# Opening loads ahead of the engines' arrivals at the barrier, and a shorter clock warm-up, in a decode attention kernel

## The chip, the cores and the metric

The kernel runs on one core of one Trainium2 chip. The metric is the device time of one execution in microseconds (us), and every number here is a device time or comes from a profile of one execution. "Span" is the time from the first to the last instruction that a profile shows; the device time is a little longer.

## The reference, cut to what matters

```python
xn = layernorm(x)                                    # x: 4 x 1 x 448
q  = (xn @ wq)                                       # 448 x 4096, 16 heads of 256
scores = einsum("bhqd,bhkd->bhqk", q, repeat(k_cache, 2)) * 256**-0.5
o  = einsum("bhqk,bhkd->bhqd", softmax(scores), repeat(v_cache, 2))
s  = o.reshape(4, 1, 4096) @ wo                      # 4096 x 448
h2 = gelu(layernorm(xn) @ w3) @ w4                   # 448 -> 1792 -> 448
out = x + s * silu(xn + h2)
```

The two caches are 4 x 8 x 8192 x 256 in bf16, 268 MB together; with the weights 279 MB are read for four output rows. (The reference's shifted branch with w1 and w2 is zero for a single position, so the kernel does not read those weights.) The caches are 32 tiles, one for each batch row and key head: 4 MB of K and 4 MB of V each.

## The kernel before

SyncE issues all large loads on one queue: wq, w3, w4, K of tiles 0 and 1, most of wo, and then K and V of the later tiles, each when its buffer comes free. ScalarE issues the load of x. A helper moves these first loads ahead of everything else on their engine, behind the instruction (a drain) with which the engine arrives at the barrier that opens the program:

```python
def begin_ahead(nc, loads):
    ...
    first = blocks[0].instructions
    for load in reversed(loads):
        at = next(n for n, i in enumerate(first)
                  if i.engine == load.engine and isinstance(i, mybir.InstDrain))
        first.insert(at + 1, load)          # behind the arrival
    blocks[0].instructions = first

def prog_sp(sp):
    ahead.append(sp.sem_inc(S["pause"], 1))     # two instructions
    ahead.append(take(sp, "pause"))             # ahead of wq
    ahead.append(sp.dma_start(vflat[1][:, 0:DK * HDH], A_wq...).then_inc(S["dwq"], 16))
    sp.dma_start(... B_w3 ...); sp.dma_start(... B_w4 ...)
    ...
    load_k(0); load_k(1)
    load_wo(NLATE, HQ, "dwo")
    for h in range(2, NH):
        load_k(h)                               # waits until tile h-2 of K is used up
        load_v(h - 2)

def prog_act(act):
    ahead.append(act.dma_start(x_sb[:, :], x2d).then_inc(S["dx"], 16))
```

TensorE first computes the small products of the prologue (q, the two layers of the MLP), then multiplies zeros to keep its clock up until the first tile of K has landed, and then works through the tiles:

```python
for i in range(NWARM):                          # NWARM = 14, the zero products
    pe.matmul(psv[0:PVW, 0:QW], pT[:, 0, 0:PVW], wq_sb[:, 0, 0:QW], start=True, stop=True)
...
def f_t(h, j):                                  # transposes of K, group j of 16
    if j == 0:
        take(pe, "dk%d" % (h % 2), 16)          # K of this tile has landed
    ...
def finish():                                   # after the last tile
    f_bc(h)
    ...                                         # rest of softmax, V of tiles 30 and 31
    f_direct(NPIECE - 1).then_inc(S["p_pv"], 1)
    take(pe, "dwl0", 16); f_o(LATE[0])
    take(pe, "v_ot");     f_o(range(HQ - REP, HQ))
    for i in range(1, len(LATE)):               # the last pieces of wo
        take(pe, "dwl%d" % i, 16)
        ins = f_o(LATE[i], i == len(LATE) - 1)
```

## Time and profile before

| | before |
|---|---|
| device time, first three runs | 653.57 us median (653.56 to 654.46) |
| profiled run: device time, span | 653.45 us, 652.0 us |
| wq issued, its first packet | 0.24 us, 1.26 us |
| x: load issued, cast starts | 0.21 us, 2.01 us |
| first tile, third K load issued | 30.07 us, 41.77 us |
| last packet of the stream | 648.80 us |

### The profile page before, as it was taken

Reading aid. Unit: us, or ns where it says so; the run is one execution under the profiler, and the core shown is the slowest. Engines: PE = TensorE matmul, PEld = TensorE weight load, DVE = VectorE, ACT = ScalarE, POOL = GpSimd, SP = SyncE. Lnnn points to the kernel's source line nnn. Section 1 sums busy time; section 2 is a strip of 40 time slices with the busy share of each in tenths; the row PEclk is TensorE's granted clock in tenths of the full one; section 3 lists DMA queues with packets and bytes.
Section 4 is the critical chain, followed back from the end, with each engine's and each line's share of the span. In section 5 each row is a group of like instructions: output and inputs, shape, how many; then the busy total and the mean of one; then the engine's idle time right before and its main releaser. Section 6 shows DMA issues by size and latency. Waiting matters only on the chain. (4 is left out here: it accounts for less than half of the span.)

```text
span 652.0 us, 22813 instructions
## 1 busy us (share of the span) xinstructions
PE 550.5 (84%) x9937; PEld 470.7 (72%) x9937; DVE 276.9 (42%) x622; ACT 255.8 (39%) x364; POOL 3.6 (1%) x17
## 2 busy tenths in 40 slices
PE   2799997988887987888897888898888798878897
PEld 1487876987676876667787766787677688757774
DVE  7344544343343443434443444444344344434442
ACT  4144543443343443323443333444234344423440
POOL 2000000000000000000000000000000000000000
PEclk9998999888799898889987888988779987978999
DMA  9999999999999999999999999999999999999997
GB/s 374 440 420 433 430 434 434 430 438 426 440 426 440 426 440 426 440 428 436 432 435 430 434 434 426 440 426 440 426 440 428 438 428 438 430 436 430 434 429 301
DMA packets 12353, 279.13 MB, mean 428 GB/s; under 512 B 1204, under 2 KB 3256, under 8 KB 3768
## 3 DMA queue, kind: packets, MB, share of 16 engines
q1 hardware_dynamic: 12328, 278.99, 99.5%
q8 instruction: 7, 0.11, 0.1%
q10 hardware_dynamic: 16, 0.01, 0.0%
q14 instruction: 2, 0.02, 0.0%
HBM read 278.99 MB, written 0.00 MB: 428 GB/s over the span
## 5 line engine op out<-in xcount | busy, mean ns | idle before, releaser
L604 PE MATMUL pst<-ident_b,kn 128*128 128x128 bf16 x4096 | 342.7, 237 | 81.4 <-PEq L278 79.3
L309 ACT ACTIVATE kT<-pst 128x1024 bf16<-128x1024 bf16 x224 | 229.3, 1024 | 357.5 <-ACTq L278 356.3
L604 PEld LDWEIGHTS pst<-ident_b,kn 128*128 128x128 bf16 x4096 | 271.7, 107 | 87.2 <-issue 86.6
L307 DVE COPY kT<-pst 128x1024 bf16<-128x1024 bf16 x288 | 197.5, 691 | 261.1 <-DVEq L278 261.1
L616 PE MATMUL psc<-qc,kT 128*128 128x2 bf16 x4096 | 178.2, 164 | 0.0
L616 PEld LDWEIGHTS psc<-qc,kT 128*128 128x128 bf16 x4096 | 157.1, 98 | 28.7 <-issue 28.5
L655 PE MATMUL psv<-vb,pT 128*4 128x512 bf16 x1056 | 85.6, 378 | 0.0
L634 PE MATMUL psm<-sel,po 128*128 128x2 f32 x272 | 36.8, 257 | 0.5 <-PEq L278 0.5
L634 PEld LDWEIGHTS psm<-sel,po 128*128 128x128 f32 x272 | 34.8, 196 | 0.9 <-issue 0.9
L655 PEld LDWEIGHTS psv<-vb,pT 128*4 128x4 bf16 x1056 | 21.8, 82 | 15.0 <-issue 0.4
L466 DVE TENSOR_REDUCE rmax<-psc 128x2 f32<-128x128 f32 x32 | 9.3, 292 | 48.1 <-DVEq L278 48.1
L484 DVE COPY po<-psv 128x512 f32<-128x512 f32 x34 | 23.5, 691 | 4.0 <-DVEq L278 3.3
L331 ACT ACTIVATE pT<-psc,negb 128x64 bf16<-128x64 f32 x66 | 20.6, 332 | 5.4 <-ACTq L278 5.4
L471 DVE TENSOR_REDUCE gmax<-psm 2x1 f32<-2x128 f32 x32 | 8.9, 279 | 32.3 <-DVEq L278 32.3
L628 PEld LDWEIGHTS psm<-diag,ones_f 2*128 2x128 f32 x66 | 13.5, 253 | 6.3 <-issue 5.0
L628 PE MATMUL psm<-diag,ones_f 2*128 2x2 f32 x66 | 16.2, 313 | 1.1 <-PEq L278 0.9
L331 ACT ACTIVATION_READ_ACCUMULATOR pT<-psc,negb 128x1 f32 x66 | 13.6, 206 | 0.0
L624 PEld LDWEIGHTS psm<-ident_f,rmax 128*2 128x2 f32 x32 | 2.6, 80 | 14.0 <-issue 14.0
L646 PE MATMUL psm<-rowsum,ones_f 128*128 128x2 f32 x64 | 11.6, 251 | 0.0
L552 PE MATMUL pst<-ident_b,xn_b 4*128 4x4 bf16 x14 | 0.6, 161 | 11.5 <-DVE xn_b L379 6.8
L646 PEld LDWEIGHTS psm<-rowsum,ones_f 128*128 128x128 f32 x64 | 9.5, 188 | 0.0
L474 DVE TENSOR_SCALAR diag<-ident_f,gmax 2x2 f32<-2x2 f32 x32 | 6.9, 217 | 4.8 <-DVEq L278 1.1
(101 smaller groups left out, 101.1 us busy)
## 6 DMA issues: line engine op xcount, KB each, us to landing
kn<-in_A_k_cache_dram SPq DMA_DIRECT2D x32, 4096.0 KB, 25.5
vb<-in_A_v_cache_dram SPq DMA_DIRECT2D x31, 4096.0 KB, 30.5
vb<-in_A_wq_dram SPq DMA_DIRECT2D x1, 3584.0 KB, 11.4
vb<-in_B_w_dram SPq DMA_DIRECT2D x2, 1568.0 KB, 16.3
wo_sb<-in_A_wo_dram SPq DMA_DIRECT2D x1, 2688.0 KB, 43.3
kn<-in_A_v_cache_dram SPq DMA_DIRECT2D x1, 2048.0 KB, 24.7
kn<-in_A_v_cache_dram SPq DMA_DIRECT2D x1, 1024.0 KB, 26.7
kn<-in_A_v_cache_dram SPq DMA_DIRECT2D x2, 512.0 KB, 27.9
```

The costliest lines, as they stand in the source:

```text
L307: engine.tensor_copy(dst, src).then_inc(S["v_ev"], 1)
L309: engine.activation(dst, src, ACT.Copy).then_inc(S["a_ev"], 1)
L331: ins = act.activation(pv_p[:, :, hh], sc[:, :, hh], ACT.Exp, bias=negb[:, s, hh:hh + 1], scale=SCALE, accum_out=rowsum[:, s, hh:hh + 1])
L466: v.tensor_reduce(rmax[:, :], psc[h % 2][:, 0:NCH * REP].rearrange("p (k h) -> p h k", h=REP), AX.X, ALU.max).then_inc(S["v_rmax"], 1)
L471: v.tensor_reduce(gmax[:, :], psm[0:REP, 0:P], AX.X, ALU.max).then_inc(S["v_s"], 1)
L484: v.tensor_copy(po[:, slot], psv[:, 0:CP * DH]).then_inc(S["v_po"], 1)
L604: ins = pe.transpose(dst[:, t * P:(t + 1) * P], kn[:, h % 2, GC * j + kl, half * P:(half + 1) * P], ident_b[:, :])
L616: ins = pe.matmul(psc[h % 2][:, kk * REP:(kk + 1) * REP], kT[:, j % RING, t * P:(t + 1) * P], qc[:, h % 2, half, :], start=(half == 0), st ...
L628: pe.matmul(psm[:, P:P + REP], ones_f[0:REP, :], diag[:, :], start=True, stop=True).then_inc(S["p_m2"], 1)
L634: ins = pe.matmul(dst(dh)[:, 0:width], po[:, slot, i * DH + dh:(i + 1) * DH:NHALF], sel[:, i, 0:width], start=(i == 0), stop=(i == CP - 1))
L646: pe.matmul(psm[:, P + REP:P + 2 * REP], ones_f[:, :], rowsum[:, h % 2, :], start=True, stop=True)
L655: ins = pe.matmul(psv[o:o + CP * REP, 0:CP * DH], pT[:, h % 2, kk * REP:(kk + CP) * REP], src[:, kk:kk + CP, :].rearrange("p c d -> p (c d)"),
```

## The change

It wants to start the stream of loads earlier: wq becomes the first instruction of SyncE, x goes ahead of ScalarE's arrival, and the two semaphore instructions that stood ahead of wq are dropped. In return for a first tile that was ready before its K, fourteen zero products become eight.

```diff
-    first = blocks[0].instructions
-    for load in reversed(loads):
-        at = next(n for n, i in enumerate(first)
-                  if i.engine == load.engine and isinstance(i, mybir.InstDrain))
-        first.insert(at + 1, load)
+    first = list(blocks[0].instructions)
+    for n, load in enumerate(loads):
+        own = [i for i in first if i.engine == load.engine]
+        drain = next(i for i in own if isinstance(i, mybir.InstDrain))
+        if n == 0:
+            later = own[0:2]
+            first = [i for i in first if i not in later]
+            at = first.index(drain)
+            first[at:at] = later
+            at = first.index(later[0])
+        else:
+            at = first.index(drain)
+        first.insert(at, load)
     blocks[0].instructions = first
...
-    NWARM = 14
+    NWARM = 8
...
         def prog_sp(sp):
-            ahead.append(sp.sem_inc(S["pause"], 1))
-            ahead.append(take(sp, "pause"))
-            ahead.append(sp.dma_start(
+            ahead.insert(1, sp.dma_start(
...
         def prog_act(act):
-            ahead.append(act.dma_start(x_sb[:, :], x2d).then_inc(S["dx"], 16))
+            ahead.insert(0, act.dma_start(x_sb[:, :], x2d).then_inc(S["dx"], 16))
```

(Left out: the name `pause` in the list of semaphores.)

More of the change, by code (lines that the diff above doesn't have):

```diff
@@ L182, in bass_recurrent_scan__gqa_block_cached__mixer_s_mlp__decode_kernel @@
         S = {n: es.enter_context(nc.semaphore(n)) for n in (
-            ["dx", "dwq", "dw3", "dw4", "dwo", "dk0", "dk1", "dv0", "dv1", "dout", "pause"]
+            ["dx", "dwq", "dw3", "dw4", "dwo", "dk0", "dk1", "dv0", "dv1", "dout"]
             + ["dvl%d" % i for i in range(NPIECE)] + ["dwl%d" % i for i in range(len(LATE))]
```

## The prediction

> **What bounds the kernel now.** I read the page first, for the share that each engine and the DMA have of the span; then the queue's own waits; then the windows and the timeline of both ends, because a bound that holds all along can only be moved where it begins or where it stops. The page's busy row and rate row for the transfers, and its memory line:
>
> ```profile
> DMA  9999999999999999999999999999999999999997
> GB/s 374 440 420 433 430 434 434 430 438 426 440 426 440 426 440 426 440 428 436 432 435 430 434 434 426 440 426 440 426 440 428 438 428 438 430 436 430 434 429 301
> ...
> HBM read 278.99 MB, written 0.00 MB: 428 GB/s over the span
> ```
>
> Only the first and the last of the 40 slices are under 400 GB/s. The 16 DMA engines are full from one end to the other, while TensorE, the busiest engine, is at 84%. The packet records say the same more sharply: from 1.37 us, as soon as the first load flows, until 648.3 us there is no stretch with fewer than eight packets in flight. 278.99 MB at the 433 GB/s of the middle (from 100 to 600 us) take 644 us; the rest of the 652.0 us span lies at the two ends. Is the queue ever short of work? SyncE's own waits:
>
> ```profile
> SPq L237 <- DVEq L515: 460.3, 30, 38.4
> SPq L245 <- DVEq L483: 132.4, 31, 19.5
> ```
>
> SyncE spends 593 us waiting for buffers to come free, and yet the stream never thins: each K load waits for VectorE to finish with a K tile, but behind loads already queued. So TensorE, VectorE and ScalarE follow the stream. The opening, in the windows view (stretch, length, busy time and count of PE, PEld, DVE, ACT, POOL, granted clock, DMA share, GB/s):
>
> ```profile
> 0.00:1.00 1.00, 0.00 (x0) 0.00 (x0) 0.08 (x1) 0.11 (x1) 0.47 (x6) 1.00 0.00 0
> 1.00:2.00 1.00, 0.00 (x0) 0.00 (x0) 0.41 (x1) 1.00 (x1) 0.77 (x6) 1.00 1.73 434
> ```
>
> Nothing moves in the first microsecond; that is the one stretch before the end in which the bound is idle, and the timeline with the instructions of the opening barrier says why:
>
> ```profile
> 0.21 0.56 ACTq L312 DMA_DIRECT2D x_sb<-in_A_x_dram  x1
> 0.24 0.41 SPq L222 DMA_DIRECT2D vb<-in_A_wq_dram  x1
> ...
> 0.78 0.34 SPq L226 DMA_DIRECT2D vb<-in_B_w_dram  x1
> ...
> 0.92 0.48 DVE L383 MEMSET pst<- 128x512 f32 x1 [0.92 <-ACTq L816]
> ...
> 2.01 0.38 DVE L385 CAST x_f<-x_sb 4x448 f32<-4x448 bf16 x1 [0.60 <-DMA x_sb<-in_A_x_dram]
> ```
>
> ```profile
> L816 SPq DRAIN  x1: 7/7/7, 0.0 to 0.0; - x1
> ...
> L220 SPq EVENT_SEMAPHORE  x1: 17/17/17, 0.1 to 0.1; - x1
> ```
>
> SyncE's arrival at the barrier is the first instruction of the span, at 0.00. It is followed by two semaphore instructions (the increment of `pause`, the wait for it) and only then, at 0.24, by the wq load that opens the stream. At the other end the chain of waits holds nothing but what follows the last piece of wo:
>
> ```profile
> 648.14 1.55 PE pst L703 x24
> ...
> 649.72 0.40 DVE res L542
> ...
> 650.13 0.38 DVE out_b L544
> ```
>
> **What the Trainium skill says.** "DMA: Bandwidth & Descriptors", section Specifications, gives 435 GB/s as the fabric ceiling; the trace's 433 in the middle agrees, so no reordering of loads can raise the rate. The same section gives some 0.6 us to the first byte for loads issued by SyncE or ScalarE; here the first packet of wq starts 1.0 us after the start of its issue, and I use that. The same page, "Issuing engines are not separate DMA queues", says that loads of different engines run on the same 16 DMA engines and interleave: so x and wq compete, and whichever comes first matters for x. "TensorE: Matmul & The Clock Gate", Part 1, says that the clock is judged over free-running windows of some 3.4 us; the trace agrees: after a stretch of 3.41 us in which TensorE was busy 2.08 us (52.04 to 55.45), the next 3.41 us were granted 0.50.
>
> **The change, part by part.**
>
> (a) *wq ahead of SyncE's arrival.* Gone are two semaphore instructions, and the arrival moves behind the load. What stood ahead of the load ends at 0.24; in the changed kernel the load is SyncE's first instruction, so it should be issued at 0.00. This lies wholly on the path: the first packet moves from 1.26 to about 1.02, every load behind it in the same queue moves along, and the end with them. Worth 0.24 us.
>
> (b) *x ahead of ScalarE's arrival.* ScalarE's first instruction starts at 0.13 (its arrival at the barrier, from the trace) and the load at 0.21, so x can be issued 0.07 us earlier. This gains nothing by itself, as x feeds only the layernorm. It may even lose: wq is now 0.13 us ahead of x, where it was 0.03 behind, and a 28 KB packet of wq took 1.6 to 2.4 us at the start. If x's four rows fall in behind such packets, the cast at 2.01 starts up to about 1.2 us later. None of that is on the path, see (d).
>
> (c) *The barrier opens later.* ScalarE now arrives after 0.56 us of issue: 0.13 + 0.56 is about 0.70, and with an arrival and its relay at about 0.08 each the release, which was at 0.61, comes at about 0.87. The first memset of VectorE (0.92) and the w3 load (0.78) slip by some 0.25 us. VectorE then waits for x in any case, and w3 is queued behind wq, which runs to 11 us. Worth 0.
>
> (d) *Eight zero products instead of fourteen.* Timeline before, around the first tile:
>
> ```profile
> 23.94 5.26 PE L596 MATMUL psv<-vb,pT 128*32 128x512 bf16 x14
> ...
> 30.07 1.05 PE L604 MATMUL pst<-ident_b,kn 128*128 128x128 bf16 x16 [0.87 <-PEq L278]
> ...
> 41.77 0.33 SPq L237 DMA_DIRECT2D kn<-in_A_k_cache_dram  x1
> ```
>
> The fourteen end at 29.2 and the first tile starts at 30.04, when its K has landed: they held up nothing. Six fewer, at a spacing of 0.43 us at half clock, end about 27.5; the gap to K (now due at 29.7) grows from 0.9 to some 2.2 us. If x is late the prologue slips by up to 1 us and that too fits in this gap, while with fourteen it would not have. So this part pays 0 directly. Its risk is the clock. A stream group of the tile repeats every 0.65 us at full clock and every 1.06 us at half clock (from the timeline around 34 and 56 us); a window of 3.41 us then does 3.2 groups instead of 5.2 and the tile ends 2.0 x 0.65 = 1.3 us later, or 2.6 us for two windows. What that would touch is the third K load, issued at 41.77 when the first tile is used up. The load of wo ahead of it in the queue writes its completions on the 16 engines between 44.0 and 45.9, and a load needs 1.0 us from issue to packets, so the room is 44.0 - 42.8 = 1.2 us on the earliest engine and 3.1 us on the last. All of these move forward by the same 0.24. One cold window just fits; two would leave the early engines idle for 1.4 us, but not the last one, on which the end depends.
>
> Sum: -0.24 + 0 + 0 + 0. From the median of 653.57 that is 653.33.
>
> **The rivals.**
>
> *The stream's start does not follow the issue.* If the first packet is set by something else (x's issue and wq's overlap in time, and either may hold up the other; the queue may need to come alive), moving the issue gains 0: 653.6. For it speaks that the small x load took 0.56 us to issue and the far larger wq only 0.41; against it, that nothing else is in flight between 0 and 1.1 us. A variant: the measured time counts from the start of the first instruction, and the engines' starts shift among each other. Then the gain is anything from 0.1 to 0.3.
>
> *The colder first tile takes the stream's room.* With two cold windows or a slipped prologue the third K load comes after the queue has emptied. For it speaks the smallest room of all loads, 1.2 us, just here; against it, that the last engine has 3.1 us. It would cost 0 to 1 us: 653.4 to 654.4.
>
> *The cold clock never comes or does not matter, and the stream gains more.* If an earlier x shortened the prologue and the first tile were gated by it, the start of the tile would move; but K's landing, not the prologue, releases it (0.87 us of waiting), so nothing further is to be had: no more than 0.3 in all, 653.25.
>
> **Range and chances.** The best estimate is 653.35: 0.24 less, a little held back for the two first rivals. The three runs before spread by 0.9 us (653.56 to 654.46), which is more than the effect; the profiled run took 653.45. The range is 652.9 to 654.1: at the bottom the full gain with some luck, at the top no gain and a run of the upper kind. 2% would be 13 us, and no part reaches even a tenth of that: faster 0.004, same 0.992, slower 0.004.
>
> **What would show it.** Right: wq's issue at 0.00 of the span; the first packets at about 1.0; the transfer rate of the windows unbroken at about 433 from then to the end; a span of about 651.8; x's cast later than 2.0, not earlier; the first tile at about 29.8, still released by K's load; a gap of 1.3 to 2.3 us between the zero products and it, perhaps with a granted clock of 0.50 in the tile; the third K load issued at most 1.5 us later than 41.5. Wrong: packets still starting at 1.2 (step a), a dip of the rate between 42 and 48 us (step d), or a first tile that waits for TensorE's own prologue.

## More of the kernel before

Part 3 lists the DMA queues with their packets, MB and share of the 16 engines, ahead of it a line on the packets in all; the kind "instruction" is an engine's program being fetched. In the kernel before:

```profile
DMA packets 12353, 279.13 MB, mean 428 GB/s; under 512 B 1204, under 2 KB 3256, under 8 KB 3768
...
q14 instruction: 2, 0.02, 0.0%
```

Queue 14 fetched twice, 8 KB each.

## The result, and the profile after

| | before | after |
|---|---|---|
| device times, same rounds | 653.56, 653.57, 654.01, 654.46 | 653.73, 654.25, 654.30, 654.76 |
| median | 653.79 us | 654.27 us |
| profiled run: device time, span | 653.45, 652.0 us | 653.73, 651.9 us |
| device time less span | 1.45 us | 1.83 us |

The ratio is 1.0006, with a 95% interval of 0.9988 to 1.0023: the same. (A ratio here is the mean time of one kernel's runs over that of the other's of the same rounds, so it is not quite the ratio of the medians quoted; for the experiments below its figures come out when the profiled runs are left out.) The direction was the surprise: 0.24 us were to be gained, and the median, 654.27, lies above the predicted range of 652.9 to 654.1.

The page of the changed kernel, the same rows as before:

```profile
GB/s 379 441 416 438 425 440 426 438 430 436 430 432 436 426 442 422 446 422 442 425 440 426 438 430 436 430 432 436 426 440 424 444 424 442 426 440 426 438 426 300
DMA packets 12352, 279.12 MB, mean 428 GB/s; under 512 B 1204, under 2 KB 3256, under 8 KB 3768
...
q14 instruction: 1, 0.01, 0.0%
HBM read 278.99 MB, written 0.00 MB: 428 GB/s over the span
```

The stream is as full as before: the first slice is a little better (379 against 374 GB/s), the last the same (300 against 301). The one line that differs in kind is queue 14, with one fetch of instructions inside the span where there were two. SyncE's own waits (line, what it waited for, us in all, times, longest) still say that it waits for buffers nearly all the time, 591 us:

```profile
SPq L243 <- DVEq L521: 458.3, 30, 37.7
SPq L251 <- DVEq L489: 132.7, 31, 18.0
```

The opening in the windows view (columns as in the prediction), and then in the timeline (start, us, engine, line, operation, tiles, and what it waited for):

```profile
0.00:1.00 1.00, 0.00 (x0) 0.00 (x0) 0.00 (x0) 0.00 (x0) 0.20 (x4) 1.00 0.00 0
1.00:2.00 1.00, 0.00 (x0) 0.00 (x0) 0.48 (x1) 0.90 (x1) 0.67 (x4) 1.00 1.87 459
```

```profile
0.00 0.41 SPq L228 DMA_DIRECT2D vb<-in_A_wq_dram  x1
0.12 0.57 ACTq L318 DMA_DIRECT2D x_sb<-in_A_x_dram  x1
...
1.11 0.33 SPq L232 DMA_DIRECT2D vb<-in_B_w_dram  x1
...
1.29 0.48 DVE L389 MEMSET pst<- 128x512 f32 x1 [1.29 <-PEq L822]
...
4.84 0.38 DVE L391 CAST x_f<-x_sb 4x448 f32<-4x448 bf16 x1 [3.06 <-DMA x_sb<-in_A_x_dram]
```

wq is issued at 0.00, and its first packet starts at 1.02 by the packet records, where it was 1.26: the first step of the prediction, to the hundredth. The windows are too coarse to show this. The price is in the last line: x is cast at 4.84 instead of 2.01, because its four packets of 896 bytes start at 2.89 to 3.37 us, behind wq's packets of 28 KB, where before they started at 1.16 to 1.61. The barrier, in the view of lines (count, shortest, median and longest in ns, first and last start):

```profile
L822 SPq DRAIN  x1: 121/121/121, 0.5 to 0.5; - x1
...
L822 POOLq EVENT_SEMAPHORE  x2: 17/17/17, 0.9 to 1.0; - x2
```

SyncE arrives at 0.5 instead of 0.0, and the barrier opens at 0.98 instead of 0.61. The first tile, in the timeline:

```profile
26.28 3.04 PE L602 MATMUL psv<-vb,pT 128*32 128x512 bf16 x8
...
29.62 1.05 PE L610 MATMUL pst<-ident_b,kn 128*128 128x128 bf16 x16 [0.30 <-PEq L284]
...
41.57 0.33 SPq L243 DMA_DIRECT2D kn<-in_A_k_cache_dram  x1
```

The whole prologue comes 2.3 us later with x (the zero products begin at 26.28, before at 23.94). Eight of them end at 29.3, and the tile starts 0.30 us later, on K's landing. Its third K load goes out 0.20 us earlier than before. And the end, from the chain of waits:

```profile
648.03 1.55 PE pst L709 x24
...
649.60 0.39 DVE res L548
...
650.02 0.38 DVE out_b L550
```

It is the same chain, each link 0.11 or 0.12 us earlier than before. So in the profiled runs the span got 0.12 us shorter by the raw records (651.88 against 652.00), and the device time 0.28 us longer. In this span there is no lost time to find. What is lost lies outside it: 1.83 us of device time that belong to no instruction of the trace, where there were 1.45.

### The profile page after: what moved, and what is told of

Its sections match the earlier page's. It is cut to its first block, busy times and chain, and to the rows that moved or that the text cites. A ratio compares the mean times of both kernels' runs of the same rounds, so it can differ in the third digit from the quotient of the medians.

```text
span 651.9 us, 22799 instructions
## 1 busy us (share of the span) xinstructions
PE 547.3 (84%) x9931; PEld 469.5 (72%) x9931; DVE 276.7 (42%) x622; ACT 255.8 (39%) x364; POOL 3.6 (1%) x17
```

## The experiments

Twelve kernels ran, in three groups of four, each group on one chip together with runs of the kernel before. Medians of the kernel before were 653.69 us in the first group, 654.39 in the second and 654.35 in the third. The third group has no fresh runs of its own to speak of: of its twelve runs of the kernel before, eleven are those of the second group, some 13 minutes earlier. Its ratios are the weaker for it. The device time less the span does not need them.

### Two controls: both kernels again

No edit. The first is the kernel before under another name; it tells how small a ratio can be believed.

> The kernel before against itself: a control for the scatter. Theory 1 (the change is worth -0.1 to -0.25 us and the miss is scatter of whole runs, 653.5 to 654.8 for either kernel): the five times spread by about 0.5 to 1 us, and its own ratio to the kernel before is off 1 by up to 0.0008, as much as the changed kernel's. Theory 2 (the change costs some 0.3 to 0.5 us): the times of this kernel lie closer together, near 653.6, and its ratio is within 0.0003 of 1. Profile in both: first packets at 1.2 to 1.3 us, x's cast at about 2.0, first tile at about 30.0.

It measured 654.56 us (653.53 to 654.94) against 653.69 for the very same program in the same rounds: a ratio of 1.0013 (1.0000 to 1.0026). Differences of about a thousandth, 0.9 us, are therefore not resolved here by medians, and this is twice the whole difference of the official result. What is steady is the device time less the span: 1.43 to 1.50 us in its five runs, 1.39 to 1.49 in the eleven of its partner.

> The changed kernel again, with more rounds. Theory 1: mean within 0.3 us of the control of the same rounds, more likely below it; first packets at 1.0, x's cast at 3.5 to 5 us because x waits behind wq, first tile at 29.6 to 29.9 all the same. Theory 2: 0.3 to 0.6 us above the control in the mean, and in the trace a stretch in which the stream runs thin, or a tail longer than the 3.2 us of before, that says where.

The changed kernel measured 654.56 us (653.84 to 655.14), ratio 1.0010 (0.9997 to 1.0023), level with the control. Its device time less its span was 1.84 to 1.89 us in four runs and 2.34 in one.

### Theory 1: the shorter program of SyncE costs 0.4 us outside the span

This difference separates cleanly. The 57 executions of kernels in which SyncE's program holds the pair of `pause` instructions have 1.38 to 1.50 us; of the 31 without it, 27 have 1.80 to 1.90 and four 2.23 to 2.34, which no run explains. (Spans are to 0.1 us, so the last digit is loose.) The packet records show what goes with it: an 8 KB fetch on queue 14 that starts 0.04 to 0.05 us before the span's end where one pair is there, and 1.11 to 1.13 us after the end where it is not. That is why the page of the changed kernel counts one. The pair is two instructions, 128 bytes; SyncE's built program is 6,272 bytes with it and 6,144 without. The rival: the order of the opening (the loads ahead of the arrivals) shifts what lies between the start of the clock and the first instruction. The two theories part when pair and order are exchanged one by one.

The kernel before without the pair, its order untouched:

```diff
         def prog_sp(sp):
-            ahead.append(sp.sem_inc(S["pause"], 1))
-            ahead.append(take(sp, "pause"))
```

> The kernel before without the pause pair; wq stays behind SyncE's arrival, so it is issued at 0.07 instead of 0.24. Theory of the shorter program: the difference of time and span is 1.85, low runs at about 653.7, slower than the kernel before although the stream starts 0.17 us earlier. Rival (the order of load and arrival costs): difference 1.45, low runs at 653.3 to 653.4. x is 0.14 us behind wq here, so its cast should be as late as in the changed kernel, 4 to 5 us, and fourteen products then end after K's landing: first tile 1 to 2 us late and some of that lost in the stream too, as in the run with wq alone moved.

The changed kernel with the pair at a place where it delays nothing, behind the issue of the wo load:

```diff
             load_wo(NLATE, HQ, "dwo")
+            sp.sem_inc(S["pause"], 1)
+            take(sp, "pause")
```

> In every run so far the measured time is longer than the trace's span by a constant: 1.39 to 1.50 us for all kernels with the pause pair on SyncE, 1.80 to 1.90 us (2.3 in a few) for all without it. The trace has an 8 KB instruction fetch starting 0.05 us before the span's end with the pair and 1.1 us after it without. Theory of the shorter program: taking the two semaphore instructions away (SyncE's program 6144 instead of 6272 bytes) shifts where SyncE stands in its fetched instructions when it reaches the end, and that costs 0.4 us after the last instruction, more than the 0.24 us gained at the start. Here the changed kernel gets the pair back at a place where SyncE only waits (behind the issue of the first wo load). Expected: difference of time and span 1.45, the late fetch at -0.05, spans as of the changed kernel (651.9 in its low kind), so low runs at 653.3 to 653.4, under the kernel before's. Rival (the wq load ahead of SyncE's arrival is what costs): the difference stays 1.85 and low runs at 653.7.

And the kernel before with a second pair there (the same edit), 6,400 bytes:

> The kernel before with a second pause pair at a place where SyncE only waits: SyncE's program is 6400 bytes, two instructions longer than before. Theory of the shorter program, as a boundary that is either met or missed: difference of time and span 1.45 again, low runs at 653.4 to 653.6. If it goes gradually with the length: 1.0 to 1.1, low runs near 653.1. If the pair's place at the start matters and not the length: 1.45.

| | pair | order of loads | median us | ratio (95%) | device time less span |
|---|---|---|---|---|---|
| before_nopause | none | old | 655.19 | 1.0008 (0.9995 to 1.0021) | 1.80 to 1.85, once 2.33 |
| after_pad | one | new | 653.50 | 0.9983 (0.9969 to 0.9998) | 1.43 to 1.48 |
| before_pad | two | old | 653.70 | 0.9990 (0.9975 to 1.0004) | 1.38 to 1.44 |

The queue line of the page of after_pad, and then that of before_nopause:

```profile
q14 instruction: 2, 0.02, 0.0%
```

```profile
q14 instruction: 1, 0.01, 0.0%
```

The difference goes with the pair in both directions and not with the order: this rival is dead. A smaller one is not tried. The kernels without the pair also name one semaphore fewer, and no run made the program longer by other instructions. With two pairs the fetch starts 29.5 us before the end and the difference stays at 1.4, so once the fetch lies inside the span, having it still earlier gains nothing. The Trainium skill, "Runtime: NRT & Kernel Launch", section Instruction fetch mechanics, says that an engine's sequencer fetches the next block of its program by its own queue while it executes the present one, and that this is mostly hidden. The traces agree for an 8 KB fetch that falls inside the span. Where it falls behind the span, the device time less the span is 0.4 us longer. That this fetch is what costs the 0.4 us, and that they lie behind the last instruction and not ahead of the first, is inferred from the two going together in all 14 traces; no run moves the fetch alone. What triggers the fetch, and what the remaining 1.4 us are, no run shows.

The lowest time of all executions is after_pad's, 653.18 us, and it is the version that I would keep: the changed kernel with these two instructions put back. Its ratio lies 0.0017 under 1, where the control lies 0.0013 over it, so it is not sure that it beats the kernel before; with its profiled run counted, its four times have a mean of 653.84 us against 654.36 for the twelve of the kernel before. What is sure is the 0.4 us outside the span, and that its spans (651.7 to 652.1 in three runs) are the changed kernel's best, give or take 0.2 us. Its fourth run, the profiled one, was a bad one: span 653.7. Most of that is not the clock. Of the 16 landings of a load, one for each DMA engine, the last falls 1.5 us further behind the eighth between 327 and 367 us, and the last packet of the stream comes at 650.06, where the changed kernel's was at 648.69. The other 0.46 us come from a tail of 3.65 us instead of 3.19, with a granted clock of 0.54 from 616.88 to 623.71 us, of which theory 3 tells more.

before_nopause also tells what the pair was good for where it stood. Without it wq is issued at 0.09, ahead of x, and x is cast at 5.02; fourteen zero products then hold the first tile up to 32.14 and the third K load to 44.38. The pair had let x go first.

### Theory 2: the three parts pay for each other, because the room at the third K load is small

The prediction gave the third K load 1.2 us of room on the earliest DMA engine and 3.1 us on the last, and held that only the last counts. The rival in it, that a colder or later first tile takes the stream's room, is tried by doing one part alone. First the zero products alone, in the kernel before:

```diff
-    NWARM = 14
+    NWARM = 8
```

> The kernel before with eight zero products instead of fourteen, nothing else: they end about 27.5, the gap to the first tile is 2.5 us. Part (d) by itself: 0 in the time, beside the same scatter of low and high runs (653.5 to 655); the first tile starts with K's landing at 30.0 and perhaps runs its first 3 to 7 us at half clock, the third K load is issued at 41.8 to 44.4, and the end stays where the last DMA engine puts it. Rival: the colder first tile thins the stream at 44 to 46 us and costs 0.3 us or more on top of the scatter.

It measured 655.67 us (654.97 to 656.50), ratio 1.0020 (1.0008 to 1.0032): the same by the 2% rule, but over 1 by more than the control, whose interval overlaps it. What was lost, and where, its trace tells better. The timeline of warm8, and one of its windows:

```profile
30.44 1.76 PE L604 MATMUL pst<-ident_b,kn 128*128 128x128 bf16 x16 [2.93 <-PEq L278]
...
43.65 0.33 SPq L237 DMA_DIRECT2D kn<-in_A_k_cache_dram  x1
```

```profile
45.00:46.00 1.00, 1.00 (x26) 0.48 (x24) 0.23 (x2) 0.00 (x0) 0.00 (x0) 1.00 0.87 309
```

The same window of the kernel before:

```profile
45.00:46.00 1.00, 1.00 (x17) 0.84 (x15) 0.55 (x3) 0.00 (x0) 0.00 (x0) 1.00 1.08 453
```

TensorE stood idle for 2.93 us ahead of the tile; the clock was halved from 30.6 to 34.0 us; the tile took longer (its first sixteen transposes 1.76 us instead of 1.05), the third K load went out at 43.65 instead of 41.77, and the stream thinned to 309 GB/s. Its last packet came at 649.66 instead of 648.80. "One cold window just fits", said the prediction; it cost 0.86 us at the stream's end. (The span of this run is 1.5 us longer than the kernel before's; the other 0.66 us are a longer tail, which is theory 3's matter.)

Now wq alone ahead of the arrival, with x behind as before and fourteen products:

```diff
-        first.insert(at + 1, load)
+        first.insert(at if load.engine == mybir.EngineType.SP else at + 1, load)
...
-            ahead.append(sp.sem_inc(S["pause"], 1))
-            ahead.append(take(sp, "pause"))
```

> Only the wq load is moved ahead of SyncE's arrival; x stays behind ScalarE's arrival, fourteen zero products stay. Theory 1: first packets at 1.0; x is 0.2 us behind wq and its cast comes at 4 to 5 us; the prologue slips by 2 to 3 us, the zero products end at about 30.6 and the first tile starts there instead of at K's landing of 29.7, about 1 us late; the third K load is issued at about 42.6, which still fits before the queue is empty (43.9 on the earliest engine, with 1 us of lead): the time is that of the changed kernel within the scatter. Theory 2 with the late x as the cost: 0.3 to 1 us slower than the control.

It measured 655.03 us (654.17 to 657.06), ratio 1.0022 (1.0008 to 1.0035), much like warm8. Some 0.4 us of it are theory 1's, since the pair is gone here too. Its timeline, and the same window:

```profile
4.67 0.38 DVE L383 CAST x_f<-x_sb 4x448 f32<-4x448 bf16 x1 [3.19 <-DMA x_sb<-in_A_x_dram]
...
26.13 5.56 PE L594 MATMUL psv<-vb,pT 128*32 128x512 bf16 x14
```

```profile
45.00:46.00 1.00, 1.00 (x23) 0.41 (x20) 0.37 (x2) 0.00 (x0) 0.00 (x0) 1.00 0.32 132
```

x is late here too, so it is wq's lead that delays x, not x's new place. The fourteen products end at 31.7 and hold the tile up to 31.63; the third K load goes out at 43.15, the stream drops to 132 GB/s, and its last packet comes at 649.56, 0.76 us late. Where the load came too late like this, the time from the issue of that load to its last landing was 13.0 us in warm8 (43.65 to 56.69) and 13.1 in wq_only (43.15 to 56.21). In the kernel before it landed at 55.61 behind a full queue. So its room, from the issue at 41.77, is 55.61 - 13.0 - 41.77 = 0.8 us on the last engine, not 3.1. That fits the kernels between: with issues at 42.11 to 42.51 (x_first, before_fill, after_pad) no such thinning shows.

The third part alone, x ahead of ScalarE's arrival:

```diff
-        first.insert(at + 1, load)
+        first.insert(at if load.engine == mybir.EngineType.Activation else at + 1, load)
```

> Only x is moved ahead of ScalarE's arrival at the barrier; wq stays behind its pause, fourteen zero products stay. Part (b) by itself: x issued at 0.13 instead of 0.21, ahead of wq, cast at 1.6 to 2.0; the barrier opens at about 0.9 to 1.0 instead of 0.6; w3 issued at about 1.1; stream from 1.2 to 1.3 us as before; time that of the kernel before within its scatter. If the late barrier were on the path: 0.3 us slower in the trace at the end of the stream (648.8 before).

It measured 653.48 us (653.41 to 654.31), ratio 0.9988 (0.9975 to 1.0001): not to be told from the kernel before. Its timeline:

```profile
0.12 0.57 ACTq L312 DMA_DIRECT2D x_sb<-in_A_x_dram  x1
...
1.69 0.37 DVE L385 CAST x_f<-x_sb 4x448 f32<-4x448 bf16 x1
```

With wq at 0.24 behind it, x is early (cast at 1.69), and w3 is issued at 1.11, as late as in the changed kernel, without the stream noticing (last packet 648.78). So the later opening of the barrier is worth 0, as predicted.

Last, the changed kernel with far too many products, to see a delay of the first tile in full:

```diff
-    NWARM = 8
+    NWARM = 40
```

> The changed kernel with 40 zero products: a dose, to test whether the queue's room at the third K load is what the prologue's length counts against. From the trace of the changed kernel the eight end at 29.0 with the clock full from 28.6; 32 more at 0.216 us end at about 36, so the first tile starts 6.4 us late, the third K load is issued at 48.0 and its packets start at 49.0, where the queue is empty from 43.9 to 45.7 (earliest to last engine). Theory 1: the end follows the last engine's gap, 49.0 - 45.7 = 3.3 us slower than the changed kernel, about 657.4; a hole of 3 to 5 us in the transfer rate between 44 and 49 us and none elsewhere. If the stream were not the bound, or other loads filled in: less than 1 us.

It measured 663.17 us (662.08 to 663.73), ratio 1.0141 (1.0126 to 1.0155). The first tile started at 36.05 and the third K load at 48.31. No packet moved between 45.43 and 49.28 us, and the load landed at 61.16, 12.9 us after its issue, 5.5 us later than in the kernel before: that is about what the issue's delay of 6.54 us less the room of 0.8 gives (5.7). The loads behind it, up to 333 us, landed 5.6 us later than in the kernel before. But the time grew by 9 us over the changed kernel where some 3.3 had been expected. The expectation counted the hole too small, for the reason just told; the other 3 us or so lie later. Between 334 and 394 us the last landings fall back by another 2.9 us, and the trace shows nine fetches of instructions on queue 8 there, where the kernel before has a single one, at 328 us; why, no run shows. And the tail behind the stream is 4.07 us instead of 3.19.

### Theory 3: the scatter of 1 us is TensorE's clock in the last tile

Both kernels' runs spread over 1 us or more. In the prediction the kernel's end followed the last piece of wo only. In the repeated run of the changed kernel (span 652.7) the chain of waits begins elsewhere:

```profile
647.46 1.10 PE pst L761 x8
...
648.96 1.46 PE pst L709 x24
```

Eight products of an earlier part of the ending (line 761, which folds the partial sums of the last V in) come first and run into the last of wo without a wait: TensorE is late itself. The windows view of the last tile, the kernel before and then this run:

```profile
616.88:623.71 6.83, 5.87 (x125) 5.78 (x125) 3.65 (x7) 4.35 (x8) 0.00 (x0) 1.00 1.02 441
```

```profile
616.88:623.71 6.83, 5.85 (x64) 5.67 (x65) 1.89 (x4) 2.55 (x6) 0.00 (x0) 0.50 0.99 427
```

At a granted clock of 0.50 TensorE is as busy and does half as much, 64 products instead of 125. The last tile's scores are then ready at 634.96 us; they were ready at 632.43 in the kernel before, without a cold window, and at 633.75 in the profiled run of the changed kernel, with one of 3.41 us. The ending after the stream takes 3.88 us instead of 3.19. So the kernel has two ends, the last of wo and TensorE's work on the last tile, and the second wins when the clock was low there.

The 14 traces bear this out to a few hundredths of a microsecond. In each trace the clock is halved for 3.41 us at a time or for two or three such stretches in a row:

| traces | half clock at the last tile | span's end after the stream's last packet | span's end after the scores |
|---|---|---|---|
| before, after, before_again, before_pad, x_first, after_fill, before_fill | none, or one stretch | 3.19 to 3.20 us | 18.12 to 19.57 us |
| after_again, after_pad, before_nopause, warm8, wq_only, after_40 | two in a row, 6.83 us | 3.65 to 4.07 us | 17.75 to 17.78 us |

(The scores count from the start of the last transpose of their maxima; the fourteenth trace is before_tail10, below.) So the span's end is the later of two times: the stream's last packet plus 3.19 us, or the scores plus 17.76. This holds for single traces of each kernel; it does not say how often which end wins.

To test it, seven products of 512 columns ahead of every tile keep TensorE busy while it waits for K, in both kernels:

```diff
-    NWARM = 8                    # the kernel before: NWARM = 14
+    NWARM, NFILL = 1, 7          # the kernel before: NWARM, NFILL = 7, 7
...
                 if j == 0:
+                    for i in range(NFILL):
+                        pe.matmul(pst[0][0:PVW, 0:512], ident_b[:, 0:PVW],
+                                  qT_all[:, 0:P].unsqueeze(1).broadcast_to([P, 4, P]),
+                                  start=True, stop=True)
                     take(pe, "dk%d" % (h % 2), 16)
```

> Theory of two ends, formed from the six traces so far: the kernel ends with the later of (i) the last wo pieces, 3.2 us before the end, and (ii) TensorE's own work on the last tile, which has 1.5 to 2 us of room. A half-clock stretch of 3.41 us inside the last tile costs 1.3 us and hides (last rmax transpose at 632.4 without one, 633.8 with one), one of 5.8 to 6.8 us costs 2.5 us and shows (635.0, and the end 0.7 us later). Which it is goes by where the free-running clock window falls, so a kernel has a low kind of run (653.5 to 653.8) and a high kind (654.2 to 655). Here seven 512-column products in the gap ahead of each tile, and one instead of eight before the first, keep TensorE busy: no or hardly any half-clock stretches after the first tile, last rmax transpose at 632.2 to 632.6, all five runs of the low kind: median 653.4 to 653.6 and a spread under 0.3 us, below the 654.5 of the changed kernel in the last job. Rival (the scatter has another cause, the transfers or the start): the spread of 1 us stays, with runs over 654.2, or the products slow every tile and the time rises by over 0.5 us.

> The kernel before with the same seven products in each gap, and seven instead of fourteen ahead of the first tile. Theory of two ends: again only low runs, median 653.5 to 653.8, spread under 0.3 us. Against the other kernel of this pair the two early loads of the change are then seen without the scatter: this one is slower by 0.1 to 0.25 us. Rival (the change costs in its own right): this one is faster than the other by 0.2 us or more.

after_fill measured 653.91 us (653.68 to 655.07), ratio 0.9994 (0.9982 to 1.0006). The mean granted clock rose from 0.906 to 0.958, and stretches at half clock fell from 122.9 us in all to 54.6. Five of its six spans lie between 651.8 and 652.1, one at 652.8; of the nine spans of the changed kernel only two do (651.9 and 652.0), the others are 652.4 to 652.9. That is what the theory wants, though the nine runs come from other rounds than the six. before_fill measured 653.73 us (653.39 to 654.52), ratio 0.9993 (0.9980 to 1.0006), with two spans at 651.9 and 652.0, one at 652.3, and two at 653.0 and 653.1. All low was expected, and that failed. Its profiled run still has a window at half clock in the last tile, from 619.3 to 622.7, so the products did not always do their work; and what the two high runs ended with no profile shows. So the spread did not go, and the clock in the last tile is one source of it, not shown to be the only one.

The counter-test makes the second end late on purpose, by ten more products of 448 columns behind the last tile, in the kernel before:

```diff
         def finish():
+            f_warm(10)
             f_bc(h)
```

> The kernel before with ten more 448-column products (0.19 us each, 1.9 us) on TensorE right behind the last tile. Theory of two ends: TensorE's room there is some 1.6 us when the last tile ran at full clock and 0.3 to 0.5 us when it had one half-clock window. So the end is now set by TensorE: +0.3 us over the low kind without a half-clock window in the last tile, +1.4 to 1.7 us with one, over 2.5 us with two; the median at 655 or more, and the chain of waits begins with the po products ahead of the last ones, not with the last wo piece. If TensorE had much room at the end: no change, 653.5 to 654.5.

It measured 655.45 us (654.22 to 655.85), ratio 1.0017 (1.0002 to 1.0031). In its profiled run the chain begins with those same eight products of the ending and the tail behind the stream is 3.84 us, so the second end is real. The median of 655 or more came as expected. The size in the trace came out smaller: its span of 652.8 is 0.7 us above that of the control with one cold window in the last tile (652.1), where 1.4 to 1.7 had been expected. The trace says why: the ten products take 2.0 us (634.21 to 636.20), but TensorE waited at this place anyway (0.94 us in the kernel before), so the end comes 18.76 us after the scores, only 1.0 more than 17.76. What the other three runs, with spans of 654.0 to 654.4, ended with no profile shows.

One more source of scatter stays open: in many traces the slowest DMA engine loses time between 320 and 370 us, 1.5 us of it in after_pad, and then stays behind to the end. Fetches of another engine's instructions on queue 8 fall there, but that is a coincidence in time, not a test.

## Why the prediction was wrong, point by point

- **The bound** was right. The stream is full in both kernels, and nothing inside it changed. (One reading is a little off: the packets in flight first fall to seven, for 0.03 us, at 647.69 and not after 648.3.)
- **(a), the issue of wq,** was right: 0.00, and the first packet at 1.02 instead of 1.26. Its worth was over-rated. At the stream's end the 16 DMA engines finish 0.19 us earlier on the mean and 0.11 on the last one, on which the end waits. The mean holds over more traces: the last load lands at 647.88 to 647.91 us on the mean of its engines in three traces with wq at 0.00 (after, after_again, after_fill), and at 648.03 to 648.14 in six with wq at 0.24; traces with a hole in the stream, and after_pad with its late engine, are left out. The last engine does not: in the same traces the last packet comes at 648.69 to 648.91 and at 648.75 to 648.99. So the lead is real, but at the end it is lost in the scatter of the slowest engine; why the mean is 0.19 and not 0.24 no run shows. The rival that the start does not follow the issue is refuted.
- **The step that failed is in the same part:** "Gone are two semaphore instructions". I counted what they had cost ahead of the load, and entered nothing for a program that is 128 bytes shorter. The missing term measured +0.4 us, in every run (1.45 to 1.83 us in the profiled ones), more than the 0.24 us that the part was to gain. The official result adds up with it: the four runs of the changed kernel have a mean span of 652.43 us. Those of the kernel before have a mean of 653.90 us of device time, which with its 1.45 us taken off is 652.45. The spans are level within 0.03 (closer than four runs that scatter by 1 us can vouch for); the means of the device time differ by 0.36 us, nearly all of it outside the span. Without the 0.4 us the median would have been about 653.87: inside the range, but still short of the gain.
- **(b), x falls in behind wq,** had the right mechanism and the wrong size: "up to about 1.2 us later" measured 2.83 (2.01 to 4.84). The term counted one wait behind a packet of wq, and there were two. x's data packets started 1.7 us later (2.89 instead of 1.16), and the four-byte packets that report their landing came another 1.1 us after the data (4.03 to 4.52), where before they followed within 0.05 us.
- **(c), the barrier,** was worth 0, as said; it opened at 0.98, not 0.87. x_first shows it alone.
- **(d), eight zero products,** was right in its outcome for this change and wrong in its reason. They "held up nothing" is true only of the kernel before. With x late, fourteen do hold up the first tile (wq_only), and with x early, eight leave a gap that the clock does not survive (warm8). The gap was predicted at 1.3 to 2.3 us and was 0.30, since the slip of the prologue took it up. The room of the third K load was mis-sized: 3.1 us by its last engine, 0.8 us by the landings, because a load that meets a queue about to run dry took 13 us to land.
- **"The chain of waits holds nothing but what follows the last piece of wo"** holds only for runs in which the clock was up in the last tile. The span of 651.8 us was met by the profiled run (651.9), not by the mean of 652.4.

## What to carry to other kernels

A change of the instruction count at an engine that does nothing but queue loads can cost or gain time outside the span (here 0.4 us for two instructions): compare device time less span first, and look at the fetches on the page's queue lines, before you look for a cause inside. A small load that everything waits for should be issued ahead of the large one that opens the stream, or be paid for by taking out later work of the same length. And measure the room of a load not by when the queue before it empties, but by how long a load takes that meets an empty queue.

## What the Trainium skill lacked or had wrong

- "Runtime: NRT & Kernel Launch", Instruction fetch mechanics, calls the fetch of a program mostly hidden. Here that depends on two instructions: with 6,144 bytes on SyncE the last 8 KB fetch starts 1.1 us after the span's end and the device time less the span is 0.4 us longer; with 6,272 or 6,400 bytes it starts inside the span and the 0.4 us are gone.
- "DMA: Bandwidth & Descriptors", Specifications, gives about 0.6 us to the first byte for loads by SyncE or ScalarE, and does not say from when. Here the first packet of wq starts 1.02 us after the start of its issue (0.00 to 1.02 and 0.24 to 1.26); the issue takes 0.41 us, so from its end it is 0.61, which agrees.
- The same section names a limit of about 358 GB/s of HBM per core, which it gets by halving a stack's 716 GB/s between two cores. It is no ceiling for a core that loads alone: this one core read at 433 GB/s for 500 us, and at 428 over the whole span.
- No page that I found gives the cost of a queue of SyncE that runs dry. In after_40 the first packets started 0.97 us after the issue (48.31 to 49.28) and took 1.2 to 2.2 us each, where later ones took 1.21, and a 4 MB load took 12.9 to 13.1 us from issue to last landing there and in warm8 and wq_only, while in a full queue such loads follow each other every 9.68 us.
- No page that I found gives what a small load loses behind a large one that was issued 0.12 us earlier: four packets of 896 bytes behind packets of 28 KB started at 2.89 us instead of 1.16.
